# The first x block of an attention and MLP kernel: rsqrt from the Sqrt table, transposes by tile, and an earlier load and LN for the second block

## The chip, the cores and the metric

The kernel runs on one core of one Trainium2 chip. The core has TensorE (PE) for matrix products and, in the same array, transposes; VectorE (DVE), ScalarE (ACT) and GpSimd (POOL) for work on elements; SyncE (SP), which issues DMAs; and 16 DMA engines. Matmul results land in PSUM[...]; everything else that is worked on lies in SBUF. The metric is the device time of one execution in microseconds, and of several runs the median counts.

## The reference

A token matrix x of 2048 x 576 is normalised; one branch is attention over the last 512 cached keys with 32 query heads on 16 key heads, the other a two-part MLP; the result is x + s * silu(mlp). Cut to what matters:

```python
xn = _layernorm(x)                       # eps 1e-5
# attention branch: Hq=32, Hkv=16, Dh=128, W=512 last keys
q = (xn @ wq).reshape(B, Sq, Hq, Dh).transpose(0, 2, 1, 3)
p = softmax(q @ k[:, :, Sk - W:].T * Dh ** -0.5)
s = (p @ v[:, :, Sk - W:]).transpose(0, 2, 1, 3).reshape(B, Sq, Hq * Dh) @ wo
# MLP branch
h  = gelu(_layernorm(xn) @ w1)
hs = shift_channel_groups(h) @ w2        # 4 groups, by +1, -1, +2, -2 tokens
x1 = xn + hs
g  = silu(x1 + gelu(_layernorm(x1) @ w3) @ w4)
return x + s * g
```

## The kernel before

The 2048 tokens are cut into four blocks of 512 (NB = 4, QB = 512), and each block into four tiles of 128 rows (TB = 4). The program has two stages. Stage A (lines 162 to 634) runs attention and the first half of the MLP, stage B (lines 637 to 755) the second half and the output. After stage B a flag is read and, if the scores could be too large, a slow path is run; on this data it is not.

Stage A is one loop over U = 128 units, a unit being one head of one block (line 616). In unit u TensorE does the first score product of head u, then the q projection of head u + 1 (`stage_q`, five matmuls at line 332 that read the transposed normalised block xT_b), then the other three score products (line 347). ScalarE turns scores into exponentials (line 349). Between those products TensorE does probabilities times V of the head before (`stage_v`, line 364); VectorE divides by the sum (lines 368 and 369) and casts q (line 337, in block 0; in later blocks ScalarE does this at line 339). SP then transposes the head's result by DMA (`stage_t`, line 377).

Other work hangs on units by hand: `at(u, fn)` puts fn into the list of unit u, `pe(u, ...)` puts matmuls there, and `later(u, make, per)` spreads the nine steps of a layernorm over units, `per` of them each. Of these the following matter here.

- A layernorm (`layernorm_steps`, line 111) is four steps of statistics (line 122 twice and line 123), one that turns four variances into 1/sqrt (`rsqrt_newton`, line 96: 11 small VectorE instructions), and four that apply (line 129).
- Layernorm 1 of block 0 runs at the start (line 606). Its input comes by four DMAs at line 253. TensorE then turns keys of head groups 0 and 1 (`prep_k`, line 237, copied out at line 241 into kT through the one bank of `ps_wo`), then the block (`tr1_first`, line 300), column group by column group through the two banks of `ps_po`. Before the keys stand 32 small matmuls on the identity (line 610).
- Layernorm 1 of a later block b + 1 is spread from unit 24 of block b on (line 576), its rows being loaded by POOL (`load_x`, line 203) at unit 14 in block 0 and at unit 4 in others (line 574). `late` puts a tiny POOL copy of a pT tile ahead of such a load, which makes POOL wait for that unit. The transposes of the result are DMAs issued by SP (`tr1`, line 298) two a unit at units 27 and 28 (line 578).
- Layernorm 2 of a block (the MLP's) is spread from unit 7, its DMA transposes into xnnT come at units 10 to 13, and the first MLP product (`b1`, line 436) at units 15 to 19.
- POOL's queue also has the loads of wq (lines 210 and 212), wo (273), keys (221) and values (227).

The order on SP, POOL and TensorE is that of the program (`manual_schedule`, line 605); on VectorE and ScalarE a scheduler arranges the instructions, and `high_priority` lets some go ahead.[...]

Stage B does 36 column groups of w3 (line 685, with Gelu at 688) and of w4 (lines 694 and 695). `finish` (line 698) adds, applies tanh, multiplies with s and stores the output (line 713, on SP) and g (line 716, on ScalarE). The last tile is computed in three column pieces of 288, 192 and 96 (line 753), and each is finished and stored by itself.

Of the kernel before, what the change touches and what calls it, by code (L numbers as in the profile page):

```python
# [8 lines left out]
P = 128  # L9
# [20 lines left out]
def kernel(  # L30
# [52 lines left out]
    ident = const.tile([P, P], BF16, name="ident")  # L83
    make_identity(nc, ident)
    flag_i = const.tile([1, 1], I32, name="flag_i")

    dram = ctx.enter_context(tc.tile_pool(name="dram", bufs=1, space=DRAM))
    s_dram = dram.tile([S, D], BF16, name="s_dram")
# [19 lines left out]
            y = y2  # L108
        return y

    def layernorm_steps(pool, dsts, srcs):
        n = len(srcs)
        hw = D // 2
        st_ = {}

        def stats(i):
            if i == 0:
                st_["mv"] = pool.tile([P, n, 2], FP32, name="ln_mv")
            st = pool.tile([P, 2, 6], FP32, name="ln_st")
            for j in range(2):  # L120
                tc.keep_in_program_order(
                    nc.vector.bn_stats(out=st[:, j, :], in_=srcs[i][:, j * hw:(j + 1) * hw]))
            nc.vector.bn_aggr(out=st_["mv"][:, i, :], in_=st[:])

        def inv():
            st_["r"] = rsqrt_newton(pool, st_["mv"][:, :, 1], n)

        def apply(i):
            nc.vector.tensor_scalar(out=dsts[i], in0=srcs[i], scalar1=st_["mv"][:, i, 0:1],
                                    scalar2=st_["r"][:, i:i + 1], op0=ALU.subtract, op1=ALU.mult)  # L130

        return ([lambda i=i: stats(i) for i in range(n)] + [inv] + [lambda i=i: apply(i) for i in range(n)])
# [29 lines left out]
    with ExitStack() as actx:  # L162
# [67 lines left out]
        def prep_k(g):  # L230
            st = {}
            src = kst_t[g // 4][:].rearrange("p a b -> p (a b)")[:, (g % 4) * W:(g % 4 + 1) * W]

            def tr(kc):
                if kc == 0:
                    st["ps"] = ps_wo.tile([P, W], BF16, name="ps_k", tag="wo")
                nc.tensor.transpose(out=st["ps"][:, kc * P:(kc + 1) * P], in_=src[:, kc * P:(kc + 1) * P],
                                    identity=ident[:, :])
                if kc == KCH - 1:
                    with tc.high_priority(offset=HP):  # L240
                        nc.vector.tensor_copy(out=kT[:, g, :], in_=st["ps"][:, :])

            return [lambda kc=kc: tr(kc) for kc in range(KCH)]
# [48 lines left out]

        def ln1_steps(b):
            xn_t[b] = xn_b[b % 2]
            return layernorm_steps(small, [xn_b[b % 2][:, tt, 0:D] for tt in range(TB)], [x[:] for x in x_t.pop(b)])

        def transpose_tile(dstT, src, tt):
            nc.sync.dma_start(out=dstT[:, :, tt * P:(tt + 1) * P], in_=src[:, tt, :], transpose=True)

        def tr1_first():  # L300
            for kc, (cst, cw) in enumerate(DCH):
                ps = ps_po.tile([P, QB], BF16, name="ps_x", tag="po")
                for tt in range(TB):
                    nc.tensor.transpose(out=ps[:, tt * P:(tt + 1) * P], in_=xn_t[0][:, tt, cst:cst + P],
                                        identity=ident[:, :])
                if kc % 2:
                    nc.scalar.activation(out=xT_b[0][:, kc, :], in_=ps[:, :], func=ACT.Copy)
                else:
                    nc.vector.tensor_copy(out=xT_b[0][:, kc, :], in_=ps[:, :])

        def tr1(b, tt):
            transpose_tile(xT_b[b % 2], xn_t[b], tt)
# [225 lines left out]
        def at(u, fn):  # L538
            fill.setdefault(u, []).append(fn)
# [17 lines left out]
        for b in range(NB):  # L557
            base = b * Hq
            if b > 0:
                for i, group in enumerate(wo_atoms(b - 1)):  # L560
                    pe(base + 1 + i, group)
            later(base + 7, lambda b=b: ln2_steps(b), 3)
            for tt in range(TB):
                at(base + 10 + tt, lambda b=b, tt=tt: tr2(b, tt))
            for c in range(5):
                pe(base + 15 + c, b1(b, c))
            for bb in ([b - 1] if b > 0 else []) + ([b] if b == NB - 1 else []):
                o2 = base + (26 if bb == b else 21)
                at(o2 - 1, lambda bb=bb: b2_shift(bb))
                for tt in range(TB):  # L570
                    pe(o2 + tt, b2(bb, tt))
                pe(o2 + 3, b2_rem(bb))
            if b + 1 < NB:
                at(base + (14 if b == 0 else 4), lambda b=b: late(pT_t[b * Hq + (14 if b == 0 else 4)][0][0:1, 0:1],
                                                                 lambda: load_x(b + 1, nc.gpsimd)))
                later(base + 24, lambda b=b: ln1_steps(b + 1), 3)
                for tt in range(TB):
                    at(base + 27 + tt // 2, lambda b=b, tt=tt: tr1(b + 1, tt))
        for i, group in enumerate(wo_atoms(NB - 1)):
            pe(U + 1 + i, group)  # L580
        at(2, lambda: late(pT_t[2][0][0:1, 0:1], load_w1))
# [21 lines left out]
        at(3 * Hq + 4, finish_flag)  # L603

        with tc.manual_schedule(engines={SP, POOL, PE}):
            for step in ln1_steps(0):
                step()
            wu = ps_sc.tile([P, QB], FP32, name="warm", tag="sc")
            for i in range(32):
                nc.tensor.matmul(wu[:, 0:P], lhsT=ident[:, :], rhs=ident[:, :], start=True, stop=True)  # L610
            for g in range(2):
                for fn in prep_k(g):
                    fn()
            tr1_first()
            stage_q(0)
            for u in range(0, max(max(fill), max(pe_fill)) + 1):
                atoms = pe_fill.get(u, []) + [fn for v, g in pe_late if v == u for fn in prep_k(g)]
                n = len(atoms)
                cut = [atoms[0:n // 3], atoms[n // 3:2 * n // 3], atoms[2 * n // 3:]]
                for i in range(4):  # L620
                    if u < U:
                        stage_s(u, i)
                    if i == 0:
                        if u + 1 < U:
                            stage_q(u + 1)
                        for fn in fill.get(u, []):
                            fn()
                        continue
                    if i < 3 and 0 <= u - 1 < U:
                        stage_v(u - 1, 2 * (i - 1))  # L630
                    for fn in cut[i - 1]:
                        fn()
                if 0 <= u - 1 < U:
                    stage_t(u - 1)


    with ExitStack() as bctx:
# [60 lines left out]
        def finish(b, tt, parts):  # L698
            t = b * TB + tt
            s_b, x_b = sx_t[b]  # L700
            for ps, lo, hi in parts:
                n = hi - lo
                bs = fin.tile([P, n], FP32, name="bs")
                for src, l0, l1 in ps:
                    nc.vector.tensor_tensor(out=bs[:, l0 - lo:l1 - lo], in0=src, in1=x1_t[b][:, tt, l0:l1], op=ALU.add)  # L705
                th = fin.tile([P, n], FP32, name="th")
                nc.scalar.activation(out=th[:], in_=bs[:], func=ACT.Tanh, scale=0.5)
                t1 = fin.tile([P, n], FP32, name="t1")
                nc.vector.tensor_tensor(out=t1[:], in0=bs[:], in1=s_b[:, tt, lo:hi], op=ALU.mult)
                o = fin.tile([P, n], BF16, name="o")  # L710
                nc.vector.scalar_tensor_tensor(out=o[:], in0=th[:], scalar=1.0, in1=t1[:], op0=ALU.add, op1=ALU.mult)
                nc.vector.tensor_tensor(out=o[:], in0=o[:], in1=x_b[:, tt, lo:hi], op=ALU.add)
                nc.sync.dma_start(out=out2[t * P:(t + 1) * P, lo:hi], in_=o[:])
                g2 = fin.tile([P, n], BF16, name="g2")
                nc.vector.scalar_tensor_tensor(out=g2[:], in0=th[:], scalar=1.0, in1=bs[:], op0=ALU.add, op1=ALU.mult)
                nc.scalar.dma_start(out=g_dram[t * P:(t + 1) * P, lo:hi], in_=g2[:])

        LA = 3
        for b in range(NB):
# [20 lines left out]
            else:  # L740
                for fc in range(FC):
                    up(b, fc, hl_pool)
                for tt in range(TB - 1):
                    for fc in range(FC):
                        down(pm, pr, fc, tt)
                    finish(b, tt, whole(tt))
                tt = TB - 1
                cuts = [0, 288, 480, D]
                for i in range(3):
                    lo, hi = cuts[i], cuts[i + 1]  # L750
                    ps = pm[TB - 1 - i][:, 0:hi - lo]
                    for fc in range(FC):
                        nc.tensor.matmul(ps, lhsT=h3_t[fc][:, tt * P:(tt + 1) * P],
                                         rhs=w4_s[fc // WS][:, fc % WS, lo:hi], start=(fc == 0), stop=(fc == FC - 1))
                    finish(b, tt, [([(ps, lo, hi)], lo, hi)])


    flag = nc.values_load(flag_i[0:1, 0:1])
# [121 lines left out]
```

## Time and profile before

| What | Value |
|---|---|
| Timed runs, us | 872.67, 874.49, 874.52, 886.79, 888.54 (median 874.52) |
| Profiled execution, us | 881.74, of which 879.9 is the span of its instructions |
| TensorE busy | 849.8 us (97%) |
| ScalarE busy | 454.7 us (52%) |
| VectorE busy | 393.8 us (45%) |
| GpSimd busy | 80.6 us (9%) |
| Mean granted TensorE clock | 0.984 |
| DMA | 83.75 MB, mean 95 GB/s |

Times in a trace are counted from the span's start. The page slices the span into 40 parts of 22 us. TensorE's share is 5 tenths in the first, 7 in the fourth (66 to 88 us) and 7 in the sixth (110 to 132 us), and 9 nearly everywhere else; VectorE's is 8 in the second and fifth. The clock granted to TensorE stands in the same slices as 6, 8 and 9 tenths in the first, fourth and seventh.

A group of the profile is read so: line, engine and operation, output <- inputs, count, then busy time and mean duration, then the engine's idle time just before the group and what ended it. A wait "PE x L1 <- DVE y L2: 5.2, 1, 5.2" says that TensorE waited 5.2 us in all, once, 5.2 at the longest, for VectorE's instruction at line 2. "issue" stands where no releaser is seen. A matmul's end is modelled, so that a run of four looks about 0.2 us longer than its starts are apart. A timeline row is start, duration, engine, line, operation, tiles, shape and count, and in brackets the idle time before it.

### The profile page before, as it was taken

The numbers are of one execution on the slowest core, as the hardware profiler recorded it, in microseconds if no ns is written. First come the engines' busy times: TensorE is split into PE (matmuls) and PEld (weight loads), VectorE is DVE, ScalarE is ACT, GpSimd is POOL, SyncE is SP. The second block draws the span as 40 slices with busy tenths as digits, with TensorE's granted clock in tenths as the row PEclk, the third lists the DMA queues.
The fourth block names the chain that finished last, engine by engine and source line by source line (L and its number), as shares of the span: only waits on it lengthen the run. The fifth ranks groups of instructions, "written<-read, shape, count | busy, mean of one in ns | idle before, by whom it ended". The sixth has DMA issues, their size and how long they took to land.

```text
span 879.9 us, 16313 instructions
## 1 busy us (share of the span) xinstructions
PE 849.8 (97%) x6508; PEld 474.4 (54%) x6508; DVE 393.8 (45%) x1221; ACT 454.7 (52%) x814; POOL 80.6 (9%) x143
## 2 busy tenths in 40 slices
PE   5996979999999999999999999999999999999996
PEld 3663645566565566565565555454444444444455
DVE  4685862156874157984134865200044017005024
ACT  1773764378886368876358875032242224225510
POOL 2341210210101101010101001000000000000000
PEclk6998999999999999999999999999999999999998
DMA  6898772247354146246138246990004004001001
GB/s 164 161 231 137 156 151 50 63 91 131 89 110 83 56 85 127 61 99 115 41 79 154 64 91 126 347 283 15 1 35 131 1 1 150 16 1 54 1 15 44
DMA packets 138675, 83.75 MB, mean 95 GB/s; under 512 B 105072, under 2 KB 131952, under 8 KB 138592
## 3 DMA queue, kind: packets, MB, share of 16 engines
q1 hardware_dynamic: 126736, 51.24, 28.8%
q0 software_dynamic: 8448, 28.15, 11.7%
q10 hardware_dynamic: 3408, 3.25, 1.1%
q8 instruction: 53, 0.87, 0.4%
q14 instruction: 30, 0.25, 0.1%
HBM read 49.17 MB, written 9.44 MB: 67 GB/s over the span
## 4 chain that ended last, share of the span: by engine, by line


## 5 line engine op out<-in xcount | busy, mean ns | idle before, releaser
L349 ACT ACTIVATE pT<-sc 128x512 bf16<-128x512 f32 x512 | 289.1, 596 | 114.2 <-PE sc L347 107.0
L347 PE MATMUL sc<-qT,kT 128*128 128x512 bf16 x512 | 183.7, 381 | 0.8 <-DVE qT L337 0.8
L685 PE MATMUL ph<-xT_b,w_s 128*128 128x512 bf16 x720 | 172.1, 379 | 0.0
L364 PEld LDWEIGHTS <-pT 128*128 128x128 bf16 x2048 | 140.0, 98 | 52.5 <-issue 1.1
L332 PE MATMUL psq<-xT_b,wq_b 128*128 128x512 bf16 x640 | 162.2, 385 | 4.9 <-issue 4.9
L688 ACT ACTIVATE h<-ph 128x512 bf16<-128x512 f32 x144 | 85.7, 596 | 155.5 <-PE ph L685 150.8
L364 PE MATMUL po<-v_sb,pT 128*128 128x129 bf16 x2048 | 162.6, 221 | 0.4 <-ACT pT L349 0.4
L694 PE MATMUL pm<-w_s,h 128*128 128x512 bf16 x540 | 145.9, 380 | 0.0
L705 DVE TENSOR_TENSOR bs<-pm,x 128x512 f32<-128x512 f32 (+3 forms) x18 | 11.1, 629 | 246.4 <-PE pm L694 198.4
L368 DVE RECIPROCAL ri<-po 128x2 f32<-128x2 f32 x256 | 42.6, 167 | 173.6 <-PE po L364 170.1
L388 PE MATMUL pswo<-wo_sb,oT 128*128 128x512 bf16 x512 | 116.5, 379 | 0.0
L369 DVE TENSOR_TENSOR o<-po,ri 128x256 bf16<-128x256 f32 x256 | 107.7, 421 | 6.3 <-DVE ri L368 0.3
L332 PEld LDWEIGHTS <-wq_b 128*128 128x128 bf16 x640 | 63.0, 99 | 80.8 <-issue 9.8
L685 PEld LDWEIGHTS <-w_s 128*128 128x128 bf16 x720 | 63.8, 98 | 73.4
L695 PE MATMUL pr<-w_s,h 128*128 128x64 bf16 x540 | 99.2, 193 | 0.0
L388 PEld LDWEIGHTS <-oT 128*128 128x128 bf16 x1024 | 65.0, 98 | 55.1
L694 PEld LDWEIGHTS <-h 128*128 128x128 bf16 x540 | 52.7, 98 | 63.7 <-issue 0.6
L339 ACT ACTIVATE qT<-psq 128x512 bf16<-128x512 f32 x96 | 57.4, 598 | 33.6 <-PE psq L332 33.6
L347 PEld LDWEIGHTS <-kT 128*128 128x128 bf16 x512 | 47.7, 98 | 29.1 <-issue 1.9
L695 PEld LDWEIGHTS <-h 128*128 128x128 bf16 x540 | 51.1, 98 | 12.2 <-issue 0.4
L210 POOL DMA_DIRECT2D wq_b<-in_A_wq_dram x30 | 23.4, 778 | 312.6 <-PE psq L332 241.1
L398 ACT ACTIVATE s_out<-pswo 128x512 bf16<-128x512 f32 x16 | 9.6, 597 | 48.2 <-PE pswo L388 48.2
(93 smaller groups left out, 508.7 us busy)
## 6 DMA issues: line engine op xcount, KB each, us to landing
wq_b<-in_A_wq_dram POOLq DMA_DIRECT2D x30, 512.0 KB, 5.3
w_s<-in_B_w_dram SPq DMA_DIRECT2D x9, 576.0 KB, 7.9
wo_sb<-in_A_wo_dram POOLq DMA_DIRECT2D x8, 576.0 KB, 4.8
w_s<-in_B_w_dram SPq DMA_DIRECT2D x9, 512.0 KB, 8.9
x_dram<-x SPq DMA_DIRECT2D x4, 576.0 KB, 3.8
x<-x_dram SPq DMA_DIRECT2D x4, 576.0 KB, 4.5
s_b<-s_dram SPq DMA_DIRECT2D x4, 576.0 KB, 6.1
x_b<-in_A_x_dram SPq DMA_DIRECT2D x4, 576.0 KB, 5.9
```

What stands on the lines that cost most here:

```text
L332: nc.tensor.matmul(psq[:, :], lhsT=w[:, kc, hh * Dh:(hh + 1) * Dh], rhs=xT_b[qb % 2][:, kc, :], start=(kc == 0), stop=(kc == NDC - 1))
L339: nc.scalar.activation(out=qT[:, :], in_=psq[:, :], func=ACT.Copy)
L347: nc.tensor.matmul(sc[:, :], lhsT=kT[:, g, kc * P:(kc + 1) * P], rhs=qT_t[u][:, :], start=True, stop=True)
L349: nc.scalar.activation(out=pT[:, :], in_=sc[:, :], func=ACT.Exp, scale=SCALE)
L364: nc.tensor.matmul(po[:, j, :], lhsT=pTs[kc][:, tt * P:(tt + 1) * P], rhs=v_sb[:, g, kc, 0:Dh + 1], start=(kc == 0), stop=(kc == KCH - 1))
L368: nc.vector.reciprocal(out=ri[:], in_=po[:, :, Dh])
L369: nc.vector.tensor_tensor(out=o[:, t0:t0 + 2, :], in0=po[:, :, 0:Dh], in1=ri[:].unsqueeze(2).to_broadcast([P, 2, Dh]), op=ALU.mult)
L388: nc.tensor.matmul(ps, lhsT=oT_t[qb * Hq + h][:, tt, :], rhs=wo_sb[:, h, lo:hi], start=(h == 0), stop=(h == Hq - 1))
L685: nc.tensor.matmul(ph[:, :], lhsT=w3[:, kc, f0:f0 + P], rhs=xT_b[b % 2][:, kc, :], start=(kc == 0), stop=(kc == NDC - 1))
L688: nc.scalar.activation(out=h3[:, :], in_=ph[:, :], func=ACT.Gelu_apprx_tanh)
L694: nc.tensor.matmul(pm[tt][:, :], lhsT=lhsT, rhs=w4[:, fc % WS, 0:M0], start=(fc == 0), stop=(fc == FC - 1))
L695: nc.tensor.matmul(pr[:, tt, :], lhsT=lhsT, rhs=w4[:, fc % WS, M0:D], start=(fc == 0 and tt == 0), stop=(fc == FC - 1), skip_group_check=True)
```

## The change

- The first layernorm (block 0) gets its 1/sqrt from ScalarE's Sqrt and one VectorE reciprocal (`rsqrt_table`). An Exp of one column, scaled by 0, follows, and waits for the reciprocal.
- The copies of head groups 0 and 1 into kT go from VectorE to ScalarE.
- `tr1_first` takes five PSUM banks at once, three of `ps_sc` and two of `ps_po`, and goes tile by tile. The copies into xT_b follow.
- Four matmuls of 512 columns on raw rows of x stand between the key transposes and the block's. Their result is not used.
- The rows of block 1 are loaded at unit 8 of block 0 instead of 14. Its layernorm starts at unit 20 instead of 24, and its four DMA transposes come one a unit at units 23 to 26 instead of two each at 27 and 28. Blocks 2 and 3 stay as they are.
- The last tile's o and g are written piece by piece into whole tiles, and each is stored once, after the third piece.

```diff
+    eps_t = const.tile([P, 1], FP32, name="eps_t")
+    nc.vector.memset(eps_t[:], LN_EPS)
...
+    def rsqrt_table(pool, var, n):
+        y = pool.tile([P, n], FP32, name="nr_y")
+        nc.scalar.activation(out=y[:], in_=var, func=ACT.Sqrt, bias=eps_t[:])
+        nc.vector.reciprocal(out=y[:], in_=y[:])
+        e = pool.tile([P, 1], FP32, name="nr_e")
+        nc.scalar.activation(out=e[:], in_=y[:, 0:1], func=ACT.Exp, scale=0.0)
+        return y
+
-    def layernorm_steps(pool, dsts, srcs):
+    def layernorm_steps(pool, dsts, srcs, rsqrt=rsqrt_newton):
...
-            st_["r"] = rsqrt_newton(pool, st_["mv"][:, :, 1], n)
+            st_["r"] = rsqrt(pool, st_["mv"][:, :, 1], n)
...
                 if kc == KCH - 1:
+                    if g < 2:
+                        nc.scalar.activation(out=kT[:, g, :], in_=st["ps"][:, :], func=ACT.Copy)
+                        return
                     with tc.high_priority(offset=HP):
                         nc.vector.tensor_copy(out=kT[:, g, :], in_=st["ps"][:, :])
...
-            return layernorm_steps(small, [xn_b[b % 2][:, tt, 0:D] for tt in range(TB)], [x[:] for x in x_t.pop(b)])
+            return layernorm_steps(small, [xn_b[b % 2][:, tt, 0:D] for tt in range(TB)], [x[:] for x in x_t.pop(b)],
+                                   rsqrt_newton if b else rsqrt_table)
...
         def tr1_first():
-            for kc, (cst, cw) in enumerate(DCH):
-                ps = ps_po.tile([P, QB], BF16, name="ps_x", tag="po")
-                for tt in range(TB):
-                    nc.tensor.transpose(out=ps[:, tt * P:(tt + 1) * P], in_=xn_t[0][:, tt, cst:cst + P],
+            pss = [(ps_sc if kc < 3 else ps_po).tile([P, QB], BF16, name="ps_x", tag="sc" if kc < 3 else "po")
+                   for kc in range(NDC)]
+            for tt in range(TB):
+                for kc, (cst, cw) in enumerate(DCH):
+                    nc.tensor.transpose(out=pss[kc][:, tt * P:(tt + 1) * P], in_=xn_t[0][:, tt, cst:cst + P],
                                         identity=ident[:, :])
+            for kc, ps in enumerate(pss):
                 if kc % 2:
                     nc.scalar.activation(out=xT_b[0][:, kc, :], in_=ps[:, :], func=ACT.Copy)
                 else:
...
-                at(base + (14 if b == 0 else 4), lambda b=b: late(pT_t[b * Hq + (14 if b == 0 else 4)][0][0:1, 0:1],
+                at(base + (8 if b == 0 else 4), lambda b=b: late(pT_t[b * Hq + (8 if b == 0 else 4)][0][0:1, 0:1],
                                                                  lambda: load_x(b + 1, nc.gpsimd)))
-                later(base + 24, lambda b=b: ln1_steps(b + 1), 3)
+                u1 = base + (24 if b else 20)
+                later(u1, lambda b=b: ln1_steps(b + 1), 3)
                 for tt in range(TB):
-                    at(base + 27 + tt // 2, lambda b=b, tt=tt: tr1(b + 1, tt))
+                    at(u1 + (3 + tt // 2 if b else 3 + tt), lambda b=b, tt=tt: tr1(b + 1, tt))
...
+            x_raw = x_t[0][0]
             for step in ln1_steps(0):
                 step()
...
             for g in range(2):
                 for fn in prep_k(g):
                     fn()
+            for i in range(4):
+                nc.tensor.matmul(wu[:, :], lhsT=ident[:, :], rhs=x_raw[:, 0:QB], start=True, stop=True)
             tr1_first()
...
         def finish(b, tt, parts):
             t = b * TB + tt
             s_b, x_b = sx_t[b]
-            for ps, lo, hi in parts:
+            o = fin.tile([P, D], BF16, name="o")
+            g2 = fin.tile([P, D], BF16, name="g2")
+
+            def part(ps, lo, hi):
...
-                nc.sync.dma_start(out=out2[t * P:(t + 1) * P, lo:hi], in_=o[:])
...
-                nc.scalar.dma_start(out=g_dram[t * P:(t + 1) * P, lo:hi], in_=g2[:])
...
+                if hi == D:
+                    nc.sync.dma_start(out=out2[t * P:(t + 1) * P, :], in_=o[:])
...
+                if hi == D:
+                    nc.scalar.dma_start(out=g_dram[t * P:(t + 1) * P, :], in_=g2[:])
+
+            for ps, lo, hi in parts:
+                part(ps, lo, hi)
+            return part
...
                 tt = TB - 1
+                part = finish(b, tt, [])
...
-                    finish(b, tt, [([(ps, lo, hi)], lo, hi)])
+                    part([(ps, lo, hi)], lo, hi)
```

## The prediction

> **What bounds the kernel now.** I read the page first: TensorE is busy 849.8 us of the 879.9 us span, so time can come only from its roughly 30 us of idleness and from stretches at half clock. The view of waits, kept to TensorE, names the idleness:
>
> ```profile
> PE ph L436 <- DMA xnnT<-xnn_b: 7.7, 1, 7.7
> PE ps_k L237 <- DVE kT L241: 5.2, 1, 5.2
> PE psq L332 <- issue: 4.9, 1, 4.9
> ```
>
> These are three single waits: the first MLP matmul of block 0 (head 15), the second K transpose at the start, and the first q projection of block 1 (issued in head 31). The view of windows shows that the two late waits also cost clock; the columns used are the stretch, its length, TensorE's busy time, and PEclk, the third figure from the end (DMA share and GB/s follow):
>
> ```profile
> 69.00:73.60 4.60, 0.00 (x0) 0.00 (x1) 0.00 (x0) 0.00 (x0) 0.00 (x0) 0.57 1.19 128
> 73.60:76.40 2.80, 2.77 (x13) 1.59 (x14) 0.00 (x0) 0.60 (x1) 0.00 (x0) 0.50 0.81 183
> ...
> 126.70:131.50 4.80, 0.00 (x0) 0.00 (x0) 0.30 (x1) 0.89 (x2) 0.00 (x0) 0.96 1.11 196
> 131.50:134.40 2.90, 2.84 (x10) 1.20 (x11) 0.00 (x0) 0.52 (x2) 0.00 (x0) 0.50 0.37 73
> ```
>
> After each wait TensorE works about 2.8 us at clock 0.50, which full clock would do in half. So the first late wait costs 7.7 + 1.4 = 9.1 us and the second 4.9 + 1.4 = 6.3 us. The start, from the timeline:
>
> ```profile
> 9.73 1.45 DVE L129 TENSOR_SCALAR xn_b<-xt,ln_mv,nr_y 128x576 bf16<-128x576 bf16 x4
> 11.10 0.42 DVE L241 COPY kT<-ps_k 128x512 bf16<-128x512 bf16 x1
> ...
> 14.20 1.01 PE L304 MATMUL ps_x<-ident,xn_b 128*128 128x128 bf16 x8 [0.52 <-DVE xT_b L309]
> ...
> 15.01 2.34 PE L332 MATMUL psq<-xT_b,wq_b 128*128 128x512 bf16 x5
> ```
>
> The K copy stands behind the whole LN on VectorE; the first q projection starts at 15.01. From there to the clock's rise at 21.8 TensorE works at 0.50.
>
> **Start, step by step.** The last statistics end at 7.53 (timeline). Before, 11 Newton instructions run from 7.56 to 9.70, 2.14 us. After, ScalarE does Sqrt on 128x4. ScalarE's tail rows are 283, 363 and 443 ns for 96, 192 and 288 columns, 0.2 us plus 0.83 ns a column, so an estimate of 0.2 us, about 0.25 with its bias operand: 7.6 to 7.85. The reciprocal takes 0.17 (the row of ri) and the four applies 1.45: xn_b is ready at 9.6 and not 11.18. That is not what TensorE then waits for. The two K copies go to ScalarE, behind the switch of table back to Exp and an Exp that waits for the reciprocal. Behind those copies stand the xT_b copies and every exp.
>
> Here a rule has to be weighed. The row of the one later switch:
>
> ```profile
> 576.83 1.28 ACT L688 ACT_TABLE_LOAD   x1 [0.51 <-ACT s_out L405]
> 578.12 1.65 ACT L688 ACTIVATE h<-ph 128x512 bf16<-128x512 f32 x3
> ```
>
> The ACTIVATE follows the load at once: 1.28 us. The Trainium skill (ScalarE: Activation LUTs, What ACT_TABLE_LOAD costs) prices a switch at about 2.66 us, as a drain of 1.38 comes on top. By the row: load 7.85 to 9.13, Exp to 9.35, K copy 0.60 (the ScalarE 128x512 row) to 9.95. By the rule the copy ends at 11.3 and the start gets 0.9 us worse than before instead of better. I take the row.
>
> TensorE then, at cold pitch (0.107 us for 128 columns, 3.46 us/32 in the first warm-up row; 0.427 for 512, four times that): K transposes 4 x 0.107 from 10.0 to 10.45, four added matmuls 4 x 0.427 = 1.71 to 12.15, twenty transposes 2.14 to 14.3. The first xT_b bank is complete at the 17th, 14.0, and its 0.42 us copy lets q start near 14.5. Now it is 15.01: a gain of **0.5 us**, of which the added matmuls have eaten 1.7. The five banks remove the 0.5 us stall at 14.20; five copies on two engines (3 x 0.42 and 2 x 0.60) keep ahead of q's 0.43 us pace.
>
> The second rule is about "kept warm". The Trainium skill (TensorE: Matmul & The Clock Gate, PE-mode transpose) says that transposes do not count as busy for the clock gate, which looks at windows of about 3.4 us. This trace has a pair to hold against it; the second figure is the busy time of TensorE, the clock rose at the end of the second window and not of the first:
>
> ```profile
> 11.60:15.02 3.42, 2.82 (x25) 2.49 (x25) 1.27 (x3) 0.80 (x2) 0.00 (x0) 0.50 0.95 212
> 15.02:18.43 3.41, 2.63 (x8) 0.83 (x7) 1.11 (x2) 0.40 (x1) 0.00 (x0) 0.50 0.00 0
> ...
> 73.04:76.45 3.41, 2.82 (x13) 1.59 (x14) 0.05 (x1) 0.60 (x1) 0.00 (x0) 0.50 0.91 179
> ```
>
> Equal busy time, transposes in the first row, mostly plain matmuls in the third. If they don't count, the added 1.71 us is half a window, the idle stretch from 6.4 to 10.0 has already dropped the clock, and it rises near 21.8 as now, so the lead of 0.5 cold us is worth 0.25 to 0.5; I take 0.3. If they did count, work would be dense from 10.0, the clock would rise near 15.0, and the third q projection, now at 22.17, would come near 18.9: a gain of 3.2. The lower end is a loss of 0.9 (the table rule).
>
> **Block 1's LN.** It leaves heads 24 to 28 for 20 to 26 on VectorE; the emitted order puts the four applies three heads (some 9 us) sooner, and the four transposes on SP one a head among the oT transposes instead of two and two. Now the last is issued at 125.73 and takes 5.7 us, to 131.4, where TensorE has wanted it since 126.7. After, it is issued by about 117 in the same clock: 5.7 us give 123, and even the worst landing of xnnT (10.7) misses by only 1 us. So the wait and its cold stretch go: **6.3 us**; ends 1 less and the full amount. What is late next there is the ScalarE copy of qT, not stalled now. On SP each transpose costs 1.25 us of issue; the oT behind it are needed only in block 1, and the four o buffers give cover of several heads. Cost on VectorE: 8 x 0.43 + 4 x 0.21 + 11 x 0.16 + 4 x 0.41 = 7.7 us go into heads where the windows show it busy 15.55 of 18.00 us (91 to 109). The order keeps every qT cast ahead of the LN pieces of its head; the cast ends some 0.9 us before its first use (casts near 104.1, scores near 105.7). A lag of about 1 us gets through as 0.3 us of TensorE idleness; ends 0 and 7.7 - 2.45 = 5.2.
>
> **The x load.** Four loads of 144 KB move from head 14 to head 8 on POOL, with their gate. There 2.2 us of POOL issue go ahead of two V loads that are wanted eight heads later: free. Where they leave:
>
> ```profile
> 62.80 1.10 POOL L203 DMA_DIRECT2D xt<-in_A_x_dram  x2 [0.40 <-DMA oT<-o]
> 64.23 1.06 POOL L203 DMA_DIRECT2D xt<-in_A_x_dram  x2 [0.33 <-DVE ri L368]
> 65.28 0.76 POOL L210 DMA_DIRECT2D wq_b<-in_A_wq_dram  x1
> ```
>
> The last xnnT transpose is issued at 62.76 and takes 10.7 us (tile view), while these loads take 6.3 to 11.0. The one before, issued at 59.17 before any x piece, took 8.8; the least is 2.6. So the fourth lands between 65.4 (no wait; TensorE arrives at 66.0) and 71.6 (a wait of 5.6). The middle, 68.5, leaves 2.5 us and, being under the 3.6 us after which the clock fell in this wait (66.0 to 69.6), no cold stretch: **6.6 us** gained. Ends: all 9.1; or nothing; or a loss of 2.6, 576 KB at the 228 GB/s of the stretch 28 to 46, if the queue at head 8 is as full.
>
> **Tail.** The last piece, 24 KB, lands 2.0 us after its issue; whole 144 KB tiles land in 1.8. The last add still ends at 874.35, so -0.2; ends +-0.4. The two earlier stores lay beside matmuls. The eps memset hides in VectorE's wait for x.
>
> **Sum.** This execution took 881.74 (span 879.9): -0.3 - 6.6 - 6.3 + 0.3 - 0.2 = -13.1, giving 868.6. The median of the timed runs, 874.52, is 7.2 below. If they have the same kernel with a shorter queue wait at head 15, the floor is common and they come to 868.6; if the profile is longer throughout, to 861.4. The timed runs spread from 872.67 to 888.54, which speaks for waits that vary, so I stay near the first: **867.0**, its own range 862 to 871.
>
> **Rivals.**
> - The clock stays up from 15.0 because transposes count: 2.9 better, 864. For: the stretch becomes dense. Against: the pair of windows. 0.15.
> - The x load isn't what delays xnnT: the third was slow without it. Only LN and start count, 6.5: 881.74 - 6.5 = 875.2 in this execution, some 870 in timed runs, with part of that wait absent. 0.20.
> - Slower: x at head 8 meets a full queue (DMA share 1.09 from 28 to 46), the backlog reaches xnnT, and a timed run's head-15 wait, about 9.1 - 7.2 = 1.9, becomes the profile's 9.1 plus 2.6: +9.8 against the 6.5, 878. It decides once this wait grows by 6.5. Against: no POOL load is issued between 45.3 and 50.3, a hole x can fill. 0.11.
> - The waits barely exist in timed runs: 874. 0.06.
> - My case: 0.48.
>
> A difference under 0.2% (1.7 us) is about what cannot be told from none. Faster: 0.48 + 0.15 + 0.20 = 0.83; same 0.06; slower 0.11. The range 861.5 to 874.5 leaves out the slower case and some of the low end.
>
> **What would show it.** In the changed profile: no wait of L332 on xT_b near head 31 and clock 1.00 there; the xnnT wait about 2.5 us; K copies on ScalarE near 9.4; q at 14.5; clock up near 21 and not 15. Wrong, if qT waits on VectorE appear between heads 20 and 26, the xnnT wait grows, or the table switch costs over 2 us.

## The result, and the profile after

| | before | after |
|---|---|---|
| Timed runs, median (lowest to highest), us | 875.51 (872.12 to 895.39), 79 runs | 870.99 (865.09 to 883.70), 42 runs |
| Profiled execution, span, us | 881.74, 879.9 | 872.25, 870.2 |
| TensorE busy, us | 849.8 | 847.6 |
| Mean granted clock | 0.984 | 0.996 |

The ratio of the times is 0.9949, with a 95% interval of 0.9935 to 0.9964: the changed kernel is faster by 4.5 us. That is inside the range and 4 us above the forecast of 867.0. Ratios leave out executions more than 1.5% over the fastest of their kernel as slow, and one profiled execution below, that of the kernel with the x load back at head 14, is such a one: 880.23 us, where its median is 869.28.

(On the page of the kernel before, TensorE's digit for the slice of 66 to 88 us, where its wait at head 15 lies, is 6 and not 7, and VectorE's 8 stands in the third and fifth slices.)

TensorE's waits, from the view of waits of the changed kernel (microseconds in all, times, longest):

```profile
PE ph L452 <- DMA xnnT<-xnn_b: 6.5, 2, 5.2
PE ps_k L247 <- ACT kT L251: 2.4, 1, 2.4
PE ps_k L247 <- DMA x<-in_A_k_cache_dram: 1.8, 1, 1.8
...
PE psq L348 <- DMA xT_b<-xn_b: 0.2, 1, 0.2
```

L452, L247 and L348 are the old L436, L237 and L332. The wait of 4.9 us for block 1's xT_b is gone; the 0.2 us of the last row lies at 391.3, in block 3. The K transposes wait 2.4 us for ScalarE where they waited 5.2 for VectorE. The first MLP product still waits 5.2 us in block 0, and it has a second wait of 1.3 in block 2 (at 335.5) that it didn't have before. The windows of the same kernel at heads 15 (the first two) and 31 (the third), columns as before:

```profile
64.00:67.38 3.38, 0.00 (x0) 0.00 (x0) 0.00 (x0) 0.00 (x0) 0.00 (x0) 1.00 1.14 300
67.38:70.80 3.42, 3.14 (x14) 1.76 (x15) 0.33 (x2) 0.60 (x1) 0.00 (x0) 0.50 0.18 37
120.00:125.00 5.00, 5.00 (x44) 3.08 (x42) 2.76 (x9) 4.51 (x9) 0.75 (x2) 1.00 1.04 173
```

At head 15 the pattern is the old one, smaller: no TensorE work, DMA full (1.14), and then 3.4 us at clock 0.50. Head 31, where TensorE stood idle from 126.7 to 131.5 before, now starts at 120.87, and block 1's first q product follows at 121.08: TensorE is busy for the whole window at clock 1.00. The start, from the timeline:

```profile
7.68 0.30 ACT L115 ACTIVATE nr_y<-ln_mv,eps_t 128x4 f32<-128x4 f32 x1 [4.72 <-DVE ln_mv L133]
7.99 1.28 ACT L118 ACT_TABLE_LOAD   x1
...
9.29 0.20 ACT L118 ACTIVATE nr_e<-nr_y 128x1 f32<-128x1 f32 x1
9.40 0.58 ACT L251 ACTIVATE kT<-ps_k 128x512 bf16<-128x512 bf16 x1
...
10.03 0.58 PE L247 MATMUL ps_k<-ident,x 128*128 128x128 bf16 x4 [2.43 <-ACT kT L251]
...
10.41 1.91 PE L633 MATMUL warm<-xt,ident 128*128 128x512 bf16 x4
...
12.11 1.60 PE L319 MATMUL ps_x<-ident,xn_b 128*128 128x128 bf16 x20
...
14.00 1.31 PE L348 MATMUL psq<-xT_b,wq_b 128*128 128x512 bf16 x5 [0.29 <-DVE xT_b L325]
```

The switch of table takes 1.28 us and the next ACTIVATE starts 0.02 after it; the K copy, the four added matmuls and the transposes start at 9.40, 10.41 and 12.11, where the prediction had them within 0.05. What it did not have is in the twenty transposes: they take 1.60 and not 2.14 us. The first seven start 0.11 us apart, the rest 0.06. The clock record says why: full clock from 12.77 on, in the midst of the transposes. Before, it came at 21.84.

Where the time of this pair went is read from the start of each head's first score product (line 347, later 363) in the two traces:

| Stretch | after minus before, us |
|---|---|
| start to head 1 (21.95 to 18.45) | -3.5 |
| wait of head 15 and its cold stretch (7.7 and 6.8 long; 5.2 and 3.4) | -2.3 |
| heads 22 to 31 | +0.4 |
| wait of head 31 and its cold stretch | -6.5 |
| later blocks, the 1.3 us wait in block 2 among them | +1.8 |
| tail (last add's end to the span's end: 5.52 to 5.98) | +0.5 |
| sum | -9.6 |

So the profiled pair shows 9.6 and the medians 4.5. The pair's before is 6 us above its median, and its head-15 wait alone is 7.7 us long. Which of these rows are the change's, and which are only what one execution happened to have, is what the experiments ask.

### The profile page after: what moved, and what is told of

Its sections match the earlier page's. It is cut to its first block, busy times and chain, and to the rows that moved or that the text cites. A ratio compares the mean times of both kernels' runs of the same rounds, so it can differ in the third digit from the quotient of the medians.

```text
span 870.2 us, 16302 instructions
## 1 busy us (share of the span) xinstructions
PE 847.6 (97%) x6512; PEld 473.3 (54%) x6512; DVE 390.8 (45%) x1210; ACT 457.3 (53%) x819; POOL 80.6 (9%) x143
## 4 chain that ended last, share of the span: by engine, by line
## 5 line engine op out<-in xcount | busy, mean ns | idle before, releaser
L348 PE MATMUL psq<-xT_b,wq_b 128*128 128x512 bf16 x640 | 159.0, 379 | 0.5 <-DVE xT_b L325 0.3
L348 PEld LDWEIGHTS <-wq_b 128*128 128x128 bf16 x640 | 62.3, 98 | 74.6 <-issue 2.8
```

The lines of the kernel that those rows point to most:

```text
L348: nc.tensor.matmul(psq[:, :], lhsT=w[:, kc, hh * Dh:(hh + 1) * Dh], rhs=xT_b[qb % 2][:, kc, :], start=(kc == 0), stop=(kc == NDC - 1))
```

## The experiments

They ran on three chips in three groups: start_only, ln_only, no_warm and wq5_later; then after_again, x_at_14, both_edits and before_wq5; then the other four. Each ratio is to the kernel before on the same chip (medians there: 876.76, 878.17 and 879.23, from 23, 29 and 29 runs). "Wait" is TensorE's wait at head 15, "head 1" the start of that head's first score product.

### The parts by themselves: start_only and ln_only

start_only is the changed kernel with x at head 14, block 1's LN at head 24 and the last tile in pieces again; only the start is new.

```diff
-                at(base + (8 if b == 0 else 4), lambda b=b: late(pT_t[b * Hq + (8 if b == 0 else 4)][0][0:1, 0:1],
+                at(base + (14 if b == 0 else 4), lambda b=b: late(pT_t[b * Hq + (14 if b == 0 else 4)][0][0:1, 0:1],
...
-                u1 = base + (24 if b else 20)
+                u1 = base + 24
...
-                    at(u1 + (3 + tt // 2 if b else 3 + tt), lambda b=b, tt=tt: tr1(b + 1, tt))
+                    at(u1 + 3 + tt // 2, lambda b=b, tt=tt: tr1(b + 1, tt))
```

> Only the start of the change: Sqrt from the table, K copies on ScalarE, five banks by tile, the four matmuls; load, layernorm of block 1 and tail as before. If the start is worth what the pair of traces shows, the second head's first score product comes near 18.5 us instead of 21.95 (3.5 sooner) and the clock rises at or before 16 us; the late waits on xnnT and xT_b stay, so the time is 2 to 4 us under before. If that was one lucky phase of the clock's windows, the clock rises near 20 and the head is 0.3 to 1 us sooner.

ln_only is the kernel before with only these two dates moved, x to head 8 and the LN to head 20.

```diff
-                at(base + (14 if b == 0 else 4), lambda b=b: late(pT_t[b * Hq + (14 if b == 0 else 4)][0][0:1, 0:1],
+                at(base + (8 if b == 0 else 4), lambda b=b: late(pT_t[b * Hq + (8 if b == 0 else 4)][0][0:1, 0:1],
...
-                later(base + 24, lambda b=b: ln1_steps(b + 1), 3)
+                u1 = base + (24 if b else 20)
+                later(u1, lambda b=b: ln1_steps(b + 1), 3)
...
-                    at(base + 27 + tt // 2, lambda b=b, tt=tt: tr1(b + 1, tt))
+                    at(u1 + (3 + tt // 2 if b else 3 + tt), lambda b=b, tt=tt: tr1(b + 1, tt))
```

> Only the x load at unit 8 and the layernorm of block 1 from unit 20; start and tail as before. Theory: the wait of the q projection near head 31 goes (4.9 to under 0.5) with its cold stretch, some 6 us in the trace, and the xnnT wait stays over 4 us. Over timed runs 2 to 4 us under before if that wait is usual in timed runs, under 1 us if it is not.

Measured: start_only 872.82 us, ratio 0.9965 (0.9938 to 0.9992); ln_only 869.73, ratio 0.9935 (0.9906 to 0.9965). Their waits, start_only first:

```profile
PE psq L348 <- issue: 4.2, 1, 4.2
...
PE ph L452 <- DMA xnnT<-xnn_b: 1.2, 2, 0.6
```

```profile
PE ps_k L237 <- DVE kT L241: 4.2, 1, 4.2
...
PE ph L436 <- DMA xnnT<-xnn_b: 1.2, 2, 0.7
...
PE psq L332 <- DMA xT_b<-xn_b: 0.3, 1, 0.3
```

Head 31 is as it should be: without the earlier LN the wait of the q product stays (start_only's first row, 4.2 us at 119.96, with a clock of 0.50 from 118.14 to 124.96); with it, it is gone, and ln_only's last row is a wait of 0.3 us at 252.4. The start is worth 2.5 us in start_only's trace (head 1 at 19.43) and about 3 in its timed runs, some ten times the 0.3 of the prediction. The rows of xnnT go against both expectations: the head-15 wait is all but gone (0.6 us), with x at head 8 and equally with x at 14. So the 7.7 us of the profile before are no fixed property of the x load's place.

### The four added matmuls: no_warm and no_warm_again

The changed kernel without the four matmuls that are to keep TensorE warm. Nothing reads their result.

```diff
-            x_raw = x_t[0][0]
...
-            for i in range(4):
-                nc.tensor.matmul(wu[:, :], lhsT=ident[:, :], rhs=x_raw[:, 0:QB], start=True, stop=True)
```

> The changed kernel without its four unused matmuls. If transposes do not count for the clock, the four matmuls raised it: without them the clock rises near 18 to 20 us, and although q starts 1.7 us sooner (near 12.3), the second head is later than the 18.45 of the changed kernel by 0.5 us or more. If transposes count, the stretch from 10.0 on is dense without them too, the clock rises by 14 to 16 us, and the second head comes within 1 us of 17.5.

> The changed kernel without its four matmuls once more, beside the other runs of this group: the median again 2 to 3 us under that of the changed kernel (some 868.5), runs spread over 863 to 877, a wait on xnnT of 0.5 to 5 us. If the four matmuls are worth their 1.7 us, the median is 871 or more.

Measured: 868.80 us, ratio 0.9905 (0.9867 to 0.9943), and in another group 870.29, ratio 0.9915 (0.9875 to 0.9955). The timeline of no_warm:

```profile
10.22 2.34 PE L319 MATMUL ps_x<-ident,xn_b 128*128 128x128 bf16 x20
...
12.64 1.60 PE L348 MATMUL psq<-xT_b,wq_b 128*128 128x512 bf16 x5
```

The transposes follow the K transposes at once, take 2.34 us because all of them are at half clock, and q starts at 12.64 and not 14.00. The clock rises at 13.40, at the end of a window (9.99 to 13.40) that holds transposes but for the last 0.76 us. Head 1 comes at 17.38, in no_warm_again at 17.81 and in both_edits at 18.02; with the four matmuls it is at 18.45 to 19.43 (after, after_again, start_only, wq5_later). So the early rise doesn't need them, and there they are about 1 us of work ahead of q. That they never help is not shown: in ln2_sooner, the fourth trace without them, the clock rose only at 19.03 and head 1 came at 19.71.

### Do transposes count for the clock? tr_alone

The changed kernel with its 32 warm-up matmuls at the very start replaced by 80 transposes of the identity, the same instruction as the block's transposes. No plain matmul comes before or among them.

```diff
-            for i in range(32):
-                nc.tensor.matmul(wu[:, 0:P], lhsT=ident[:, :], rhs=ident[:, :], start=True, stop=True)
+            wt = ps_po.tile([P, QB], BF16, name="warmt", tag="po")
+            for i in range(80):
+                nc.tensor.transpose(out=wt[:, 0:P], in_=ident[:, :], identity=ident[:, :])
```

> The changed kernel with its 32 first matmuls replaced by 80 transposes of the identity, 8.5 us at 0.107 each. If transposes do not count for the clock, all 80 run 0.107 us apart and the clock does not rise in them. If they count, the clock rises within two windows, 3.4 to 6.9 us, and those after it are 0.056 us apart. Its time is read for nothing else.

Measured in a single execution: 876.16 us, with a head-15 wait of 7.2; the question is for the trace. Two views of the tile, for the time up to 5.7 and after it (count, duration least/median/most in ns, first and last start):

```profile
L629 PE MATMUL warmt<-ident x39: 284/314/314, 1.6 to 5.6; 128*128 128x128 bf16 x39
...
L629 PE MATMUL warmt<-ident x44: 219/219/314, 5.4 to 8.0; 128*128 128x128 bf16 x44
```

(The two overlap by the few at the border.) In the first, 38 steps fill 4.0 us, 0.106 us each; after the rise the starts are 0.055 to 0.057 us apart. The clock record rises at 5.74. Transposes by themselves raised the clock: they count. In this trace the clock then stayed up through the start, and head 1 came at 17.27, the earliest of all, though the four matmuls are in it: the 80 transposes end at 8.2, in time in which TensorE otherwise waits for the most part.

### What delays xnnT: wq5_later, before_wq5, both_edits, x_at_14

In the changed kernel's trace the last xnnT transpose is issued at 59.42 and lands at 67.53, 8.1 us later, with no x piece beside it: the x pieces were issued from 41.36 and had all landed by 46.94. But POOL's next load, wq for heads 20 to 23, had moved up. Before, it stood behind x at 65.28; now it is issued at 58.96 and lands at 66.81. That suggested that it had only taken x's place. wq5_later issues it two heads later:

```diff
-            at(4 * (j - 1) - 1, lambda j=j: load_wq(j))
+            at(17 if j == 5 else 4 * (j - 1) - 1, lambda j=j: load_wq(j))
```

> The changed kernel with the wq load of heads 20 to 23 issued at unit 17 instead of 15. If that load has taken the place of the moved x load beside the last xnnT transpose, the transpose lands within 5 us of its issue and the wait of the first MLP matmul falls from 5.2 to 2 us or less, the clock stays at 1.00, and timed runs are 2 to 4 us under the changed kernel. If the transposes are slow by themselves or behind the keys and values loaded before, the wait stays over 4 us.

before_wq5 has the same edit in the kernel before; both_edits is no_warm with it.

> The kernel before with nothing but the wq load of heads 20 to 23 moved from unit 15 to 17. If that load is what makes the xnnT wait, it falls under 2 us here too though the x load stays at unit 14, and timed runs are 2 to 5 us under before. If x and wq each are enough to slow the transposes, the wait stays at 3 us or more and the time within 1 us of before.

> The changed kernel without its four matmuls and with the wq load at unit 17. If the two gains add (1.7 us at the start, or 1 us as far as traces show; and the calm queue at head 15), the median comes to 863 to 864.5 us, under the 865.25 of the wq edit alone, with a xnnT wait under 2 us and a first q projection before 13 us. If the start's lead is lost at head 15 because TensorE only arrives earlier at the same landing, it stays at 865 to 866.

x_at_14 is the changed kernel with only x's load put back (the first edit of start_only's diff), and after_again is the changed kernel once more beside it.

> The changed kernel with the x load back at unit 14, the layernorm still from unit 20. If the earlier x load is what the change gains at head 15, the xnnT wait grows to 7 us or more and timed runs are 2 us or more over the changed kernel. If the wq load takes the place of x, so that the two are as bad, timed runs stand within 1 us of the changed kernel, and the xnnT wait is in its range of 1 to 6 us.

> The changed kernel once more, so that its runs stand beside the others of this group. If the wait on xnnT varies from run to run, the runs spread over 865 to 878 us again and this trace shows a wait other than 5.2 us; if it is fixed, the wait is 5.2 us again within 0.5.

| Kernel | x at head | wq load moved | wait, us | median (range), us | ratio (95%) |
|---|---|---|---|---|---|
| after_again | 8 | no | 2.5 | 871.67 (865.77 to 882.97) | 0.9949 (0.9914 to 0.9985) |
| wq5_later | 8 | yes | 1.1 | 865.25 (864.11 to 867.24), 6 runs | 0.9880 (0.9848 to 0.9912) |
| both_edits | 8 | yes | 1.1 | 868.25 (863.61 to 876.88) | 0.9898 (0.9864 to 0.9931) |
| x_at_14 | 14 | no | 14.2, in an execution of 880.23 us | 869.28 (866.46 to 880.23), 7 runs | 0.9894 (0.9856 to 0.9933) |
| before_wq5 | 14 | yes | 0.5 | 878.55 (873.69 to 888.36) | 1.0009 (0.9973 to 1.0045) |

wq5_later looked like the answer: a short wait, the best median and a spread of 3 us. Two runs speak against it. In the kernel before the same edit brought nothing (1.0009), though the wait of that one trace was short; and in both_edits the spread came back to 13 us, at a ratio no better than no_warm's without the edit (0.9898; 0.9905 and 0.9915). So the narrow 865 of six runs is not confirmed as the edit's, and the wq load is not shown as the cause. It is not excluded either: with it moved, the wait is 0.5 to 1.1 us in all three traces, and of the nine others with layernorm 2 in its place seven have over 2 us. Nor is x shown: in x_at_14's trace the last xnnT transpose took 16.8 us and the wait was 14.2, but that execution is 11 us over its kernel's median, and start_only and before_wq5, with x at 14 too, waited 0.6 and 0.5. In timed runs the kernel with x at 14 is not slower than the one with x at 8; if anything it is faster (0.9894 against 0.9949), but its interval ends at 0.9933, where that of all 42 runs of the changed kernel begins at 0.9935, and it rests on few runs.

### Take the wait away from the other side: ln2_sooner and before_ln2

If the transposes into xnnT land late now and then, they can be issued sooner. ln2_sooner is no_warm with layernorm 2 and its transposes three heads earlier in every block; before_ln2 is the kernel before with the same edit.

```diff
-            later(base + 7, lambda b=b: ln2_steps(b), 3)
+            later(base + 4, lambda b=b: ln2_steps(b), 3)
...
-                at(base + 10 + tt, lambda b=b, tt=tt: tr2(b, tt))
+                at(base + 7 + tt, lambda b=b, tt=tt: tr2(b, tt))
```

> The changed kernel without its four matmuls, and with the MLP's layernorm and its xnnT transposes three units sooner in every block (units 4 and 7 on instead of 7 and 10). Theory: what is left of the spread is the landing of the last xnnT transpose, which had some 3 us before TensorE wants it and now has some 12. Then no wait on xnnT over 0.3 us is left in any block, the clock stays up from about 14 us to the end, and timed runs draw together at 862 to 866 us. If the spread comes from something else, it stays at 863 to 877.

> The kernel before with the MLP's layernorm three units sooner and nothing else. The wait on xnnT near head 15 goes; the wait of the q projection near head 31 stays at 4 to 5 us, with its cold stretch, as does the start. If the xnnT wait is usual in timed runs, the median falls by 2 to 5 us, to 872 to 874; if it was a rarity of the profiled execution, by under 1 us.

Measured: ln2_sooner 876.57 us, ratio 0.9998 (0.9970 to 1.0026), beside no_warm_again's 870.29 on the same chip, so worse by about 6 us; before_ln2 873.68, ratio 0.9969 (0.9936 to 1.0001). Neither trace has a head-15 wait. In before_ln2 no other wait took its place, and its twelve runs spread over 7 us (871.79 to 878.71), where the 29 of the kernel before on the same chip spread over 22; that fits a wait that comes and goes in the kernel before, but the interval reaches 1. The view of waits of ln2_sooner begins with a new one:

```profile
PE po L380 <- DVE o L385: 6.7, 2, 3.4
```

and its timeline of VectorE has what that instruction waited for:

```profile
63.25 0.42 DVE L385 TENSOR_TENSOR o<-po,ri 128x256 bf16<-128x256 f32 x1 [5.32 <-DMA oT<-o]
...
71.09 0.42 DVE L385 TENSOR_TENSOR o<-po,ri 128x256 bf16<-128x256 f32 x1 [5.88 <-DMA oT<-o]
```

VectorE may not write the next o until the DMA transpose of an old one has read it. In this stretch oT transposes took up to 18.0 us to land and the last xnnT 17.3 (issued 50.81, landed 68.15). TensorE then waited twice for 3.4 us, with the clock at 0.50 from 63.41 to 66.82 and from 70.23 to 77.06. Here the delay of the transposes did not go away; another consumer met it. All twelve runs of ln2_sooner lie between 874.38 and 879.86, so it is not one execution's loss; that this wait is the whole of it is not shown, nor why before_ln2 is free of it.

## Why the prediction was right or wrong, point by point

**The sign and the range** held: faster, given 0.83, and 870.99 between 861.5 and 874.5. The sum was off in two of its terms, in opposite directions (in the pair the start gave 3.2 us more than was booked and head 15 4.3 less), so that the forecast came this near is in part luck.

**Block 1's LN: right.** Predicted 6.3 us, 6.5 in the pair. The head-31 wait is absent from the traces that have the earlier LN and is 4.2 to 5.1 us long in the three without it that were taken for experiments (start_only, before_wq5, before_ln2). ln_only moves x as well; that the LN's date alone suffices, only x_at_14's long execution shows, which has no such wait with x at 14. Of the price on VectorE, 0.3 was taken of 0 to 5.2; heads 22 to 31 are 0.4 longer, and no wait on qT appears there.

**The start: the term that was mis-sized.** The schedule of events was right (but the first bank is complete at the 16th transpose, not the 17th), and so was the choice of the row of 1.28 us for the table switch: the Trainium skill's 2.66 (ScalarE: Activation LUTs, What ACT_TABLE_LOAD costs) would, as an estimate, have put the K copy at 10.8, and it came at 9.40. What failed is the step "if they don't count, ... it rises near 21.8 as now, so the lead of 0.5 cold us is worth 0.25 to 0.5; I take 0.3". The clock rose at 12.77, and the start gave 3.5 in the pair. In the traces with the new start and its four matmuls head 1 lies at 18.45 to 19.43 (after, after_again, start_only, wq5_later), and with the old start at 20.23 to 22.19 (before, ln_only, before_wq5, before_ln2): the means, 18.95 and 21.58, are 2.6 apart, so the pair's 3.5 is at the lucky end. This is the first rival's mechanism, to which the text gave 0.15 and 3.2 us.

The Trainium skill's rule behind it (TensorE: Matmul & The Clock Gate, PE-mode transpose: transposes don't count as busy in the way that other matmuls do) is contradicted by tr_alone. The pair of windows that seemed to agree with it was misread. Its 2.82 us of busy time from 11.60 to 15.02 rest on modelled ends, which reach into the gaps. By their starts the transposes come every 0.107 us but for two stalls that add 0.30 and 0.72 us, so the window is filled for about 2.4 of 3.42 us, 70%. The row below it in the prediction (15.02 to 18.43) has five q products of 0.427 and 0.31 us of a score product: 2.44 us, 71%, all plain matmuls, and the clock didn't rise at its end either. The row that raised it (73.04 to 76.45) is filled to 83%, by starts too. It was the stalls and not the kind of instruction. The changed kernel's window from 9.36 to 12.77, at the end of which the clock rose, is filled from 10.03 on, for 2.7 us or 79%. Counted so at the start of all fourteen traces, in steps of 3.41 us back from the clock records, no window filled to 74% or less raised the clock, and every one filled to 79% or more did. Where the windows lie differs between executions, and a window's border can cut a dense stretch in two: the old start had the rise at 16.76 in before_wq5, and the new one, in ln2_sooner, only at 19.03, after a window of 70%.

**The x load: not confirmed.** The step "the fourth lands between 65.4 ... and 71.6 ... The middle, 68.5, leaves 2.5 us", worth 6.6, rests on the x pieces being what delays the last xnnT. In the pair this wait went from 7.7 to 5.2 us, and 2.3 were gained. But the wait is 7.7, 0.6 and 0.5 us in traces with x at 14 (before, start_only, before_wq5) and 5.2, 2.5, 0.6, 3.8, 5.4 and 7.2 with x at 8 (after, after_again, ln_only, no_warm, no_warm_again, tr_alone): it varies from execution to execution, at either place of x (to 14.2 in x_at_14's long one), and x's place doesn't explain it. Whether the wq load has a part is open. The text's second rival, "the x load isn't what delays xnnT" (0.20, some 870 us in timed runs), describes this best. That the hole in POOL's queue at head 8 could take x was right: the four pieces landed 3.9 to 4.4 us after their issue. The slower rival did not come about: the kernel as a whole is faster.

**The tail: nothing.** Predicted -0.2, and +0.5 in the pair. From the last add's end to the span's end takes 5.52 to 6.34 us in the five traces with pieces and 5.40 to 6.10 in the nine with a whole tile: the same.

**From the profiled execution to the median.** The text asked whether timed runs have the same kernel with a shorter head-15 wait. Profiled executions do. The changed kernel's two traces, after and after_again, are 4.0 us apart, and the difference of their waits (5.2 and 2.5) with the first one's cold stretch (3.4 us at half clock) is 4.4. How much of the spread of timed runs is this wait no run shows, as they have no trace; but the changed kernel's runs over 875 us all have a mean clock of 0.986 to 0.992 and those under 867 one of 0.995 to 0.999, so the long ones have more cold time. A term that counts on removing such a wait in one profiled execution can't be carried to a median, and of the forecast 7.5 us 4.5 came. The parts alone gave about 3 (start) and 5.7 (dates of x and LN) in timed runs, with some 2.5 of interval on each side, more together than the 4.5 of the whole. Whether that excess is chance or a cost of the parts together is open.

**What stays open:** what makes DMA transposes land in 5 us in one execution and in 8 to 17 in another between 50 and 75 us. Two things go with it in the twelve traces with layernorm 2 in its place; both were found afterwards and are not tested. The last xnnT transpose landed in 4.6 to 4.9 us in the five where GpSimd issued no load within 0.7 us of it (ln_only, start_only, before_wq5, wq5_later, both_edits), and in 6.2 to 16.8 in the seven where it issued one, x or wq. And the load of keys 6 to 8 us ahead of it had already taken 6.1 to 7.2 us in six of those seven (5.8 in tr_alone), and 5.3 to 6.0 in the five. But ln2_sooner's took 17.3 us with the nearest load 0.8 us away.

Without the four matmuls the kernel is probably better than the changed one: the three series without them that leave layernorm 2 in place (no_warm twice, both_edits) have 0.9905, 0.9915 and 0.9898 against 0.9949, though two of these intervals reach into the changed kernel's. The shortest profiled spans, 862.5 and 863.7, are both_edits' and wq5_later's; the shortest timed run of all, 862.73 us, is no_warm's.

## What to carry to other kernels

Before a profiled wait is booked as a gain, look whether it is in other executions too: a wait of 7.7 us on a DMA that shares its engines was 0.5 us in a sibling's trace. Count a clock window by the starts of the instructions, not by modelled ends; transposes counted here like other matmuls. Filler put ahead of useful work cost its own length here, while in tr_alone 80 transposes in time that was mostly idle kept the clock up. When a late transfer is asked for sooner, look who else queues with it: in ln2_sooner the o buffers waited instead.

## What was not expected of the hardware

- Transposes raised the clock by themselves: 39 at a pitch of 0.106 us, then 0.056, with the record at 5.74 us (tr_alone).
- The clock is granted in windows of about 3.41 us whose place differs between executions: the rise in block 0 came at 21.84 and 21.97 (before, ln_only), but at 16.76 and 23.05 (before_wq5, before_ln2) with the same start code. Windows filled to 70, 71 and 72% did not raise it (11.60 to 15.02 and 15.02 to 18.43 before; 2.53 to 5.94 after, which the warm-up fills to 4.98), windows filled to 79 and 83% did. The fullest that didn't, of all traces, is 74% (both_edits, 0.70 to 4.11); where between 74 and 79% the limit lies no run here shows.
- A DMA transpose of o, always of the same size, took from 2.4 us (after, issued at 71.09) to 18.0 us (ln2_sooner, issued at 52.98) to land.
